# Nine zero products instead of 13 at TensorE's first place, and another order table, in a fused attention and max-of-three expert kernel

## The chip, the cores and the metric

The kernel runs on one core of a Trainium2 chip. The metric is the device time of one execution in microseconds; the time before is the median of three runs. One execution was also taken by the hardware profiler, and all rows below are of that one.

In the rows PE is TensorE (its products), PEld its weight loads, DVE is VectorE, ACT is ScalarE, POOL is GpSimd and SP is SyncE, which here only issues transfers. L719 is line 719 of the kernel.

## What is computed

Causal attention for 4 batches of 12 heads (448 tokens, 64 numbers a head), and then, for all 1792 tokens, the largest of three products with weight matrices, times an output matrix:

```python
scores = scale * np.matmul(q, k.transpose(0, 1, 3, 2))
scores = np.where(mask, -1000000000.0, scores)
scores = scores - np.max(scores, axis=-1, keepdims=True)
attn = np.exp(scores)
attn = attn / (np.sum(attn, axis=-1, keepdims=True) + 1e-09)
attn_out = np.matmul(attn, v)
...
x = attn_out.transpose(0, 2, 1, 3).reshape(B * S, H * D)
h = np.maximum(np.maximum(x @ w1, x @ w2), x @ w3)
return h @ w_out
```

## The kernel before

**Attention.** The 48 heads are taken as 24 pairs, six to a batch, and each pair's causal scores in two halves (7 blocks of 64 queries: three blocks in half a, four in half b). A half passes through these steps, each recorded once by a helper with its own line:

- L719, PE: scores into `S` (two buffers, `S0` for halves a and `S1` for halves b), 10 or 12 products in 32 bits, after a mask written as a small product.
- L743, DVE: the largest score of each row, one reduction a block into `acc`.
- L751 or L753: these, scaled, as the bias of the exponential, on ACT, DVE or POOL.
- L761, ACT: one exponential a block, from `S` into a staging tile (`region0`), with the row sums beside it.
- In the first six pairs (batch 0, "plain"): L774, PE transposes the result into `M` (three buffers), L541 on ACT moves it out of `M`; L901, PE spreads the inverse row sums into `M`; L847, PE multiplies with the values into `O`; L906 and L541 write `x`, the experts' input.
- In later pairs the exponentials are split in two 16-bit halves (L541 on ACT, L543 and L552 on DVE or POOL), transposed by a transfer (L829), and multiplied at L847.

**Weights.** Each of the 24 blocks of 128 rows is loaded (L935), brought into a 32-bit tile (L541 or L545), given its bound (L953, L950, L956, L960 on DVE) and split into two 16-bit halves (L541 or L545, and L561). L642 and L561 do the like for the values.

**Experts.** Batches 0 and 1 take L1041 (three products of 18 each for a column block, the largest of them kept at L1056) and L1472 (the output product). Batches 2 and 3 together take a scheme with seven products for eight (L1273, folds at L1286), whose sums and splits DVE prepares (L1126, L1131, L1317, L561, L543), and end with L1398, folds at L1414 and L1430, and stores.

**The order.** Each step is handed to a recorder (`add`) with the engines that may take it and a planned cost. `ORDER` lists the 1,973 steps by number in the order in which they are placed, and `ENGINE` names for each step the engine that takes it, two letters a step. The planner (`forward`) gives each a planned start by these two tables, and the steps are then issued in the order of planned starts, engine by engine. An engine runs its list strictly in that order, so the tables decide both who does a step and what stands ahead of it. The planner keeps PE's planned starts half a microsecond behind their inputs from planned time 90 on (`PAD`, `PAD_FROM`).

**The start.** Before the recorded steps, L1528 clears a tile `junk`, and L1532 multiplies it with itself into `S0`, 13 times, 384 columns each. Nothing reads the result. The first scores come next on PE; they need the first load of `qk` (L698, on SP's queue), the first thing that SP issues.

Of the kernel before, what the change touches and what calls it, by code (L numbers as in the profile page):

```python
# [34 lines left out]
ORDER = [15, 16, 17, 18, 19, 28, 29, 20, 977, 978, 50, 21, 30, 31, 32, 33, 0, 24, 22, 983, 23, 85, 2, 34, 979, 4, 6, 35, 51,  # L35
# [166 lines left out]
class Order:  # L202
# [89 lines left out]
    def forward(self, prio):  # L292
# [25 lines left out]
        while ready:  # L318
            cand = []
            for i in [ORDER[len(placed)]] if ORDER else ready:  # L320
                o = ops[i]
# [121 lines left out]
def attention_moe(ctx: ExitStack, tc: tile.TileContext, both_, v, w1, w2, w3, wo, out):  # L443
# [1087 lines left out]
    for _ in range(13):  # L1531
        PE.matmul(buf["S"][0][:, 0:384], junk[:, 0:P], junk, start=True, stop=True)  # L1532
# [86 lines left out]
```

## Time and profile before

| | |
|---|---|
| median of 3 runs | 436.81 us |
| the runs | 436.71, 436.81, 437.38 us |
| the profiled execution's own time | 436.95 us |
| its span, first to last instruction | 434.9 us |
| PE busy | 424.0 us, 97% |
| DVE busy | 400.0 us, 92% |
| ACT busy | 300.4 us, 69% |

The span lies 2.05 us below the time of the same execution; what lies around the span is not in the rows. Busy time counts an instruction from its recorded start to its recorded end, and where instructions overlap, once. The recorded ends of PE are modelled, and an instruction's recorded time on ACT or DVE is some tenth of a microsecond longer than the step from its start to the next one's, so steps from start to start are the price of one in a row.

### The profile page before, as it was taken

The page shows a single profiled execution, that of the slowest core. Times are in us where ns is not written, and L with a number is a line of the kernel's source. Part 1 is how long each engine was busy: PE and PEld are TensorE (multiplying, and loading weights), DVE is VectorE, ACT ScalarE, POOL GpSimd, SP SyncE. Part 2 cuts the span into 40 slices and gives each one's busy share as a digit, 9 for nine tenths or more (in the row PEclk, how much of TensorE's full clock was granted, in tenths as well). Part 3 has the DMA queues.
Part 4 walks back from the last instruction along what each step waited for, and adds up shares of the span by engine and source line. Part 5 has one row for each costly group of instructions (what it writes and reads, how often), then busy time and mean ns, then how long its engine had stood idle before and what let it go on. Part 6 is the DMA issues. An engine that isn't in the chain of part 4 may idle for free.

```text
span 434.9 us, 10858 instructions
## 1 busy us (share of the span) xinstructions
PE 424.0 (97%) x4286; PEld 245.4 (56%) x4286; DVE 400.0 (92%) x850; ACT 300.4 (69%) x738; POOL 119.9 (28%) x123
## 2 busy tenths in 40 slices
PE   7899899999999999999999999999999999999997
PEld 3677665656655555555555555555555555555554
DVE  4999999999999999986657889999999999999994
ACT  4999999799879899987679887964323422431530
POOL 2234443235451515232232332110130121131000
PEclk9999999999999999999999999999999999999999
DMA  8685589999999588476977567661000000000024
GB/s 314 209 310 176 207 238 245 221 232 211 253 246 247 181 222 161 93 161 110 200 162 173 138 142 121 98 133 51 2 0 21 2 1 23 0 2 0 2 98 155
DMA packets 87490, 60.46 MB, mean 139 GB/s; under 512 B 76304, under 2 KB 79504, under 8 KB 87440
## 3 DMA queue, kind: packets, MB, share of 16 engines
q1 hardware_dynamic: 83904, 48.14, 46.3%
q10 hardware_dynamic: 3536, 11.63, 8.0%
q8 instruction: 33, 0.54, 0.5%
q14 instruction: 17, 0.14, 0.1%
HBM read 35.39 MB, written 5.51 MB: 94 GB/s over the span
## 4 chain that ended last, share of the span: by engine, by line
PE 90%; ACT 8%; DVE 1%; issue 1%; POOL 0%; POOLq 0%; ACTq 0%
PE M L1041 29%; PE L L1273 14%; PE M L1472 10%; PE S L719 8%; PE O L847 7%; PE M L1273 7%; PE L L1398 5%; ACT region L761 4%; PE O L1273 4%; ACT region L541 2%; PE M L1398 2%; PE M L901 1%; PE O L1398 1%; ACT junk L642 1%; PE S L1532 1%; PE M L774 1%
## 5 line engine op out<-in xcount | busy, mean ns | idle before, releaser
L1041 PE MATMUL M<-x,w 128*128 128x448 f16 x648 | 127.1, 353 | 0.0
L1041 PEld LDWEIGHTS <-w 128*128 128x128 f16 x648 | 61.5, 98 | 56.8 <-issue 1.7
L761 ACT ACTIVATE region<-S,acc 128x128 f32<-128x128 f32 (+6 forms) x168 | 78.4, 480 | 10.2 <-DVE region L552 3.2
L743 DVE TENSOR_REDUCE acc<-S 128x1 f32<-128x320 f32 (+6 forms) x168 | 62.6, 414 | 10.6 <-PE S L719 9.3
L541 ACT ACTIVATE region<-region 128x896 f16<-128x896 f32 (+3 forms) x72 | 57.7, 809 | 20.9 <-DVE region L1206 7.9
L552 POOL TENSOR_TENSOR region<-region 128x896 f16<-128x896 f32 x22 | 41.6, 1890 | 53.2 <-DVE region L953 14.0
L1273 PEld LDWEIGHTS <-region 128*128 128x128 f16 x324 | 31.7, 98 | 29.6
L541 ACT ACTIVATE region<-region,cols 128x384 f16<-128x384 f32 (+1 forms) x38 | 22.5, 612 | 35.3 <-DVE region L1131 26.2
L1126 POOL TENSOR_TENSOR region<-w 128x384 f32<-128x384 f16 x21 | 19.0, 913 | 96.1 <-PE L L1273 24.9
L719 PE MATMUL S<-region 64*64 64x192 f32 (+6 forms) x672 | 43.8, 379 | 0.0
L1472 PE MATMUL M<-h,w 128*128 128x448 f16 x216 | 42.2, 353 | 0.0
L847 PE MATMUL O<-region,region 128*64 128x128 f16 (+3 forms) x1320 | 41.0, 219 | 0.0
L1273 PE MATMUL L<-region,region 128*128 128x448 f16 x189 | 37.7, 352 | 0.0
L1273 PEld LDWEIGHTS <-w 128*128 128x128 f16 x243 | 23.6, 98 | 21.9
L761 ACT ACTIVATION_READ_ACCUMULATOR region<-S,acc 128x1 f32 x168 | 35.6, 212 | 0.0
L1273 PE MATMUL M<-x,w 128*128 128x448 f16 x162 | 33.0, 353 | 0.0
L541 ACT ACTIVATE region<-region,acc 128x448 f32<-128x448 f32 (+6 forms) x59 | 28.4, 513 | 5.7 <-DVE acc L810 5.7
L1472 PEld LDWEIGHTS <-w 128*128 128x128 f16 x216 | 20.7, 98 | 19.5 <-issue 0.6
L719 PEld LDWEIGHTS S<-region 64*64 64x64 f32 x672 | 24.5, 134 | 10.7 <-issue 8.6
L847 PEld LDWEIGHTS <-region 128*64 128x64 f16 x1080 | 26.6, 111 | 5.5 <-issue 5.2
L956 DVE SCALAR_TENSOR_TENSOR region<-region 128x768 int32<-128x768 int32 x24 | 23.0, 961 | 0.0
L960 DVE SCALAR_TENSOR_TENSOR region<-region 128x768 int32<-128x768 int32 x24 | 22.7, 951 | 0.1
(174 smaller groups left out, 736.5 us busy)
## 6 DMA issues: line engine op xcount, KB each, us to landing
region<-in_moe_w_dram SPq DMA_DIRECT2D x12, 768.0 KB, 4.7
region<-in_qk_dram SPq DMA_DIRECT2D x19, 448.0 KB, 4.5
region<-in_moe_w_dram ACTq DMA_DIRECT2D x6, 768.0 KB, 4.7
region<-in_v_dram SPq DMA_DIRECT2D x10, 384.0 KB, 6.0
region<-in_moe_w_out_dram SPq DMA_DIRECT2D x4, 768.0 KB, 5.6
region<-in_qk_dram ACTq DMA_DIRECT2D x5, 448.0 KB, 3.5
out_dram<-osb SPq DMA_DIRECT2D x10, 224.0 KB, 2.4
region<-in_moe_w_out_dram ACTq DMA_DIRECT2D x2, 768.0 KB, 5.0
```

The lines of the kernel that those rows point to most:

```text
L541: ACT.activation(o, i, AF.Copy, scale=f)
L552: ENG[eng].tensor_tensor(out=o, in0=i, in1=hi, op=ALU.subtract)
L719: PE.matmul(ap(o, dims[0], dims[1:], D * (h ^ g), D), l, r, start=start, stop=True, skip_group_check=True)
L743: DVE.tensor_reduce(out=T(acc)[:, at : at + 1], in_=T(S)[:, c : c + w], op=ALU.max, axis=AX.X, negate=True)
L761: ACT.activation(T(y)[:, c : c + w], T(S)[:, c : c + w], AF.Exp, bias=T(acc)[:, 16 + at : 17 + at], scale=0.125, accum_out=T(acc)[:, 8 + a ...
L847: PE.matmul(o, vt(j, vl, (2 * p + h) * D), i, start=n < 2, stop=True, skip_group_check=True)
L956: DVE.scalar_tensor_tensor(out=xi(), in0=word(0), scalar=29, in1=xi(), op0=ALU.logical_shift_right, op1=ALU.bitwise_or)
L960: DVE.scalar_tensor_tensor(out=xi(), in0=word(1), scalar=SIGN, in1=xi(), op0=ALU.bitwise_and, op1=ALU.bitwise_or)
L1041: PE.matmul(T(M)[:, 0:S_LEN], w16[j][:, kk, wl, fs], xx[:, kk % 3, xl], start=(kk == 0 and wl + xl == 0), stop=(kk == 5 and wl == 1))
L1273: PE.matmul(T(M)[:, 0:S_LEN], stat(c, wl), mov(c, xl), start=first and n == 0, stop=n == 8, skip_group_check=True)
L1398: PE.matmul(T(M)[:, t[0] : t[1]], stat[0](c, wl), mov[0](c, xl)[:, t[0] : t[1]], start=first and c + wl + xl == 0, stop=c == 2 and wl == 1 ...
L1472: PE.matmul(T(M)[:, 0:S_LEN], w16[3][:, f, wl, es], T(("h", b, f))[:, hl], start=(f == 0 and hl + wl == 0), stop=(f == 5 and wl == 1))
```

## The change

The loop at L1532 runs nine times instead of 13, and the two tables have new values. The recorded steps, their planned costs and all other code are the same. (The middle of both tables is left out.)

```diff
-ORDER = [15, 16, 17, 18, 19, 28, 29, 20, 977, 978, 50, 21, 30, 31, 32, 33, 0, 24, 22, 983, 23, 85, 2, 34, 979, 4, 6, 35, 51,
...
+ORDER = [15, 16, 17, 18, 19, 977, 28, 20, 21, 50, 29, 24, 30, 978, 22, 23, 31, 32, 979, 26, 33, 980, 34, 35, 0, 36, 983, 51,
...
     ACT.activation(osc[:, 0:1], junk[:, 0:1], AF.Exp)
-    for _ in range(13):
+    for _ in range(9):
         PE.matmul(buf["S"][0][:, 0:384], junk[:, 0:P], junk, start=True, stop=True)
```

What the tables do to the engines' lists is shown at two places. The first is ACT's list around the exponentials of half a of the seventh pair (`acc0`, `S0`; the 43rd to 45th of 168), whose end frees `S0` for half a of the eighth pair. The row above them is the last exponential of the sixth pair. Before:

```order
L761 ACTIVATE region0_61,acc1_67<-S1_92,acc1_67 128x192
L541 ACTIVATE region4_65<-M1_89,bsc_101 128x448
L892 ACTIVATE acc1_67<-acc1_67,osc_100 128x8
L541 ACTIVATE region1_62<-region1_62 128x768
L761 ACTIVATE region0_61,acc0_66<-S0_91,acc0_66 128x448
L761 ACTIVATE region0_61,acc0_66<-S0_91,acc0_66 128x384
L761 ACTIVATE region0_61,acc0_66<-S0_91,acc0_66 128x64
```

Now:

```order
L761 ACTIVATE region0_61,acc1_67<-S1_92,acc1_67 128x192
L751 ACTIVATE acc0_66<-acc0_66,osc_100 128x3
L541 ACTIVATE region0_61<-M0_88 128x512
L892 ACTIVATE acc1_67<-acc1_67,osc_100 128x8
L761 ACTIVATE region0_61,acc0_66<-S0_91,acc0_66 128x448
L761 ACTIVATE region0_61,acc0_66<-S0_91,acc0_66 128x384
L761 ACTIVATE region0_61,acc0_66<-S0_91,acc0_66 128x64
```

The weight tile's step of 768 columns (`region1`) has moved behind these exponentials, and a bias of three columns, which DVE or POOL had before, stands ahead of them.

The second is PE's list where the first expert products (L1041) stand. The scores above them are those of half b of the seventh pair (`S_92`) before:

```order
L719 MATMUL S_92<-region_65 64x128 x2
L719 MATMUL S_92<-region_65 64x256 x2
L719 MATMUL S_92<-region_65 64x320 x2
L719 MATMUL S_92<-region_65 64x192 x2
L901 MATMUL M_90<-ident,acc_67 64x64 x14
L1041 LDWEIGHTS w_0_93
L1041 MATMUL M_89<-x_68,w_0_93 128x448
```

and those of half a of the eighth (`S_91`), one half further, now:

```order
L719 MATMUL S_91<-region_65 64x448 x2
L719 MATMUL S_91<-region_65 64x384 x2
L719 MATMUL S_91<-region_65 64x64 x2
L774 MATMUL M_89<-ident,region_61 128x128 x4
L1041 LDWEIGHTS w_1_94
L1041 MATMUL M_90<-x_68,w_1_94 128x448
```

The first expert products have moved behind one more half of scores and the last transposes of batch 0.

## Rows read from the trace of the kernel before

**Rows 1.** The page: busy time of each engine, with its share and its instructions.
```profile
PE 424.0 (97%) x4286; PEld 245.4 (56%) x4286; DVE 400.0 (92%) x850; ACT 300.4 (69%) x738; POOL 119.9 (28%) x123
```

**Rows 2.** Busy time by stretch; after the bounds their length, then each engine.
```profile
core 0: us, PE busy (x) PEld busy (x) DVE busy (x) ACT busy (x) POOL busy (x), PEclk, DMA share, GB/s
5.00:10.00 5.00, 3.15 (x50) 1.79 (x52) 3.37 (x10) 2.15 (x10) 1.21 (x2) 1.00 1.00 408
...
10.00:50.00 40.00, 35.32 (x584) 27.14 (x577) 39.16 (x92) 39.82 (x122) 15.66 (x22) 1.00 0.67 223
50.00:432.00 382.00, 381.74 (x3649) 214.68 (x3647) 356.26 (x738) 256.94 (x608) 101.85 (x92) 1.00 0.53 126
300.00:420.00 120.00, 120.00 (x636) 62.04 (x634) 119.02 (x218) 44.47 (x78) 20.36 (x22) 1.00 0.02 7
...
200.00:220.00 20.00, 20.00 (x264) 11.71 (x262) 12.36 (x34) 15.04 (x46) 3.71 (x6) 1.00 0.93 180
220.00:240.00 20.00, 20.00 (x248) 11.75 (x247) 13.15 (x29) 16.26 (x44) 6.58 (x6) 1.00 0.70 162
```

**Rows 3.** PE's waits over the span: for whom, us in total, times, longest.
```profile
PE M L774 <- ACT region L761: 2.4, 2, 1.7
PE M L774 <- ACT region L541: 1.2, 3, 0.8
```

**Rows 4.** The chain that ended last: start, length, what.
```profile
9.23 2.21 ACT region L761 x11
...
49.77 0.66 PE M L774 x4
...
54.26 1.24 PE M L1041 x6
```

**Rows 5.** Timeline of the first microseconds: start, length, what, idle before it.
```profile
0.79 0.40 SPq L698 DMA_DIRECT2D region<-in_qk_dram  x1
...
1.18 4.33 PE L1532 MATMUL S<-junk 128*128 128x384 f16 x13 [1.18 <-DVE junk L1528]
...
4.36 0.15 PEld L1532 LDWEIGHTS <-junk 128*128 128x128 f16 x1 [0.17 <-issue]
4.68 0.15 PEld L1532 LDWEIGHTS <-junk 128*128 128x128 f16 x1 [0.17 <-issue]
...
5.50 0.96 PE L719 MATMUL S<-region 64*64 64x448 f32 x12
...
6.56 2.41 DVE L743 TENSOR_REDUCE acc<-S 128x1 f32<-128x448 f32 x7 [4.67 <-PE S L719]
```

**Rows 6.** Transfers issued from 0.5 to 1.2 us: size, us to landing.
```profile
region<-in_qk_dram SPq DMA_DIRECT2D x1, 448.0 KB, 3.5
```

**Rows 7.** Timeline of ACT alone, 44 to 58 us.
```profile
44.19 1.01 ACT L541 ACTIVATE region<-region,bsc 128x768 f16<-128x768 f32 x1
45.02 0.71 ACT L761 ACTIVATE region<-S,acc 128x448 f32<-128x448 f32 x1
...
52.21 0.41 ACT L892 ACTIVATE acc<-acc,osc 128x8 f32<-128x8 f32 x1
52.40 1.04 ACT L541 ACTIVATE region<-region 128x768 f32<-128x768 f32 x1
53.25 0.71 ACT L761 ACTIVATE region<-S,acc 128x448 f32<-128x448 f32 x1
...
54.61 0.30 ACT L761 ACTIVATION_READ_ACCUMULATOR region<-S,acc 128x1 f32 x1
```

**Rows 8.** Timeline of PE alone, 49 to 58 us.
```profile
55.48 0.96 PE L719 MATMUL S<-region 64*64 64x448 f32 x12
56.43 1.18 PE L774 MATMUL M<-ident,region 128*128 128x128 f32 x8
```

**Rows 9.** DVE's instructions by line and form: busy, mean ns, idle before.
```profile
L561 DVE SCALAR_TENSOR_TENSOR w<-region,wf,w 128x768 f16<-128x768 f32 x22 | 22.0, 1006 | 0.0
...
L543 DVE TENSOR_SCALAR osb<-M,osc 128x448 f32<-128x448 f32 x3 | 2.0, 682 | 3.3 <-PE M L1472 3.3
```

More of the change, by code (lines that the diff above doesn't have):

```diff
@@ L33 @@
 V_FIRST = 14
-ORDER = [15, 16, 17, 18, 19, 28, 29, 20, 977, 978, 50, 21, 30, 31, 32, 33, 0, 24, 22, 983, 23, 85, 2, 34, 979, 4, 6, 35, 51,
[93 rows of a table removed]
+ORDER = [15, 16, 17, 18, 19, 977, 28, 20, 21, 50, 29, 24, 30, 978, 22, 23, 31, 32, 979, 26, 33, 980, 34, 35, 0, 36, 983, 51,
[93 rows of a table added]
     1972]
 ENGINE = (
-    "spacspdvspacpospacdvpedvdvdvdvsppedvdvdvacacacacpeacpeacpedvdvdvdvdvacacacacpeacpeacpeacdvpeacdvacposppedvdvdvac"
-    "acacacpeacpeacpedvdvdvdvpoacacacacpeacpeacpepodvpeacdvacposppedvdvdvpoacacacpeacpeacpedvdvdvdvdvacacacacpeacpeac"
-    "pepodvpeacdvacposppedvdvdvpoacacacpeacpeacpedvdvdvdvpoacacacacpeacpeacpeacdvpeacdvacposppedvdvdvpoacacacpeacpeac"
-    "pedvdvdvdvacacacacacpeacpeacpepodvpeacdvacposppedvdvdvpoacacacpeacpeacpedvdvdvdvdvacacacacpeacpeacpeacdvpeacdvac"
-    "pospacspacspacspacdvpedvdvdvdvacdvacdvacdvpoacdvsppedvdvdvdvacacacacposppedvdvdvdvacacacacacacposppepeacdvpeacdv"
-    "acposppedvdvdvacacacacacposppedvdvdvdvacacacacacacposppepepodvpeacdvacposppedvdvdvacacacacacposppedvdvdvdvacacac"
-    "acacacposppepeacdvpeacdvacposppedvdvdvacacacacacposppedvdvdvdvdvacacacacacposppepeacdvpeacdvacposppedvdvdvpoacac"
-    "acacposppedvdvdvdvacacacacacacposppepeacdvpeacdvacpoacpedvdvdvacacacacacposppedvdvdvdvacacacacacacposppepeacdvpe"
-    "acdvacpospacacacspacacacdvpedvdvdvdvacpoacdvacdvacdvacacspacspacspacdvpedvdvdvdvacpoacdvpodvpodvdvacpedvdvdvacac"
-    "acacacdvacacacacdvsppedvdvdvdvpoacacacacacdvacacacacacposppepeacdvsppedvdvdvacacacacacdvacacacacposppedvdvdvdvac"
-    "acacacacdvdvacacacacacposppepedvdvacpedvdvdvacacacacacdvacacacdvposppedvdvdvdvpoacacacacpodvacdvacdvacposppepeac"
-    "dvsppedvdvdvdvacacacpodvacdvacacposppedvdvdvdvdvacacacacacdvdvacdvdvdvdvsppepedvdvsppedvdvdvdvacacacpodvacacacac"
-    "dvsppedvdvdvdvacacacacacpodvacdvdvdvacposppepeacdvacpedvdvdvdvacacacpodvacdvdvdvdvsppedvdvdvdvacacacacacacdvacdv"
-    "acacacdvsppepeacdvsppedvdvdvpoacacacacdvacdvdvacdvsppedvdvdvdvpoacacacacacdvdvacacacdvposppepeacdvsppedvdvdvpoac"
-    "acacdvdvacacdvacdvsppedvdvdvdvacacacacacacdvacacacacacdvsppepeacdvacpedvdvdvacacacacacdvacacacacdvsppedvdvdvdvac"
-    "acacacacpodvdvacdvdvacposppepeacdvsppedvdvdvacacacacdvdvacacdvdvdvsppedvdvdvdvacacacacacpodvdvdvacdvdvposppepeac"
-    "dvsppedvdvdvdvacacacacdvacdvacdvdvsppedvdvdvdvpoacacacacdvdvacacacacacdvsppepeacdvsppedvdvdvdvacacacacdvacacacac"
-    "dvsppedvdvdvdvacacacacacdvdvdvacacacacdvsppepeacdvsppodvdvdvdvsppodvdvdvdvsppodvdvdvdvpedvdvdvdvdvpodvpodvpoposp"
-    "podvdvdvdvsppodvdvdvdvspacdvdvdvdvpedvdvdvdvdvacdvacdvpodvspacdvdvdvdvspacdvdvdvdvspacdvdvdvdvpedvdvdvdvdvacdvac"
-    "dvacdvacacdvdvdvdvspacdvdvdvdvacacdvdvdvdvpedvdvdvdvdvacdvacdvacdvacacdvdvdvdvacacdvdvdvdvspacdvdvdvdvpedvdvdvdv"
-    "dvacdvacdvacdvacacdvdvdvdvspacdvdvdvdvacacdvdvdvdvpedvdvdvdvdvacdvacdvacdvspacdvdvdvdvacacdvdvdvdvacacdvdvdvdvpe"
-    "dvdvdvdvacdvacdvacpospacdvdvdvdvspacdvdvdvdvspacdvdvdvdvpedvdvdvdvacdvdvdvdvdvdvacacacacacacpepepeacpepepedvpepe"
-    "pedvacpopepepeacpepepedvpepepedvacpopepepeacpepepedvpepepedvacpopepepeacpepepedvpepepedvacpopepepeacpepepedvpepe"
-    "pedvacpopepepeacpepepedvpepepedvacpodvpepepedvsppepepeacsppepepedvsppepepeacsppepepeacsppepepeacacpepepeacpepepe"
-    "dvpepepedvacdvpepepeacpepepedvpepepedvacdvpepepeacpepepedvpepepedvacpopepepeacpepepedvpepepedvacdvpepepeacpepepe"
-    "dvpepepedvacdvpepepeacpepepedvpepepedvacpodvpepepeacsppepepeacsppepepeacsppepepeacacpepepedvacpepepeacacdvdvpopo"
-    "dvpodvdvacdvacdvpodvacdvacdvdvdvpodvdvdvacdvacdvdvpoacdvacdvdvdvdvdvdvdvacdvacdvdvdvacdvacdvdvdvdvdvdvdvacdvacdv"
-    "dvdvacdvacdvdvdvdvdvdvdvacdvacdvdvdvacdvacdvdvdvdvdvdvdvacdvacdvpodvacdvacdvpodvdvpodvdvacdvacdvdvdvacdvacdvpopo"
-    "podvdvdvacdvacdvdvdvacdvacdvdvdvdvpodvdvacdvacdvdvdvacdvacdvpopodvdvdvdvacdvacdvpodvacdvacdvpodvpodvdvdvacdvacdv"
-    "podvacdvacdvpodvdvdvdvdvacdvacdvdvdvacdvdvdvpopopopodvdvacdvacdvdvdvacdvacdvdvpopodvdvdvacdvacdvdvdvacdvacdvpodv"
-    "podvdvdvacdvacdvdvdvacdvacdvpeacpedvpedvpedvpedvpepedvdvpeacpedvpedvpedvpedvpepedvdvdvdvdvpeacpedvpedvpedvpedvpe"
-    "pedvdvdvdvdvdvdvacdvacdvdvdvdvacdvacdvdvdvdvacdvpeacpedvpeacpedvpedvpepedvdvpeacpedvpedvpedvpedvpepedvdvdvdvdvpe"
-    "acpedvpedvpedvpedvpepedvdvdvdvdvacdvacdvacdvdvdvdvacdvacdvacdvdvdvdvpeacpedvpeacpedvpedvpepedvdvpeacpedvpedvpedv"
-    "pedvpepedvdvdvdvdvpeacpedvpedvpedvpedvpepedvdvdvdvdvacdvacdvacdvdvdvdvacdvacdvacdvdvacdvdvpepeacpepedvpepeacsppe"
-    "pedvpepedvacpepedvacpepedvacpepeacpepedvpepeacacpepedvpepedvacpepedvsppepedvsppepeacpepedvpepeacsppepedvpepedvsp"
-    "pepedvspdvpepedvsppepedvsp")
@@ new lines @@
+    "spacspdvspacpospacdvpedvdvdvdvsppedvdvdvacacacacpeacpeacpedvdvdvdvpoacacacacpeacpeacpedvdvpeacdvacposppedvdvdvac"
+    "acacacpeacpeacpedvdvdvdvpoacacacacpeacpeacpepodvpeacdvacposppedvdvdvpoacacacpeacpeacpedvdvdvdvpoacacacacpeacpeac"
+    "peacdvpeacdvacposppedvdvdvpoacacacpeacpeacpedvdvdvdvacacacacacpeacpeacpeacdvpeacdvacposppedvdvdvpoacacacpeacpeac"
+    "pedvdvdvdvdvacacacacpeacpeacpeacdvpeacdvacposppedvdvdvpoacacacpeacpeacpedvdvdvdvdvacacacacpeacpeacpeacdvpeacdvac"
+    "pospacspacspacspacdvpedvdvdvdvpodvacdvacdvpoacdvsppedvdvdvacacacacacposppedvdvdvdvpoacacacacacposppepeacdvpeacdv"
@@ new lines @@
+    "acposppedvdvdvacacacacacposppedvdvdvdvdvacacacacacposppepeacdvpeacdvacposppedvdvdvpoacacacacposppedvdvdvdvacacac"
+    "acacacposppepeacdvpeacdvacposppedvdvdvpoacacacacposppedvdvdvdvacacacacacacposppepeacdvpeacdvacpoacpedvdvdvacacac"
+    "acacposppedvdvdvdvacacacacacacposppepeacdvpeacdvacpoacpedvdvdvdvacacacacposppedvdvdvdvpoacacacacacposppepeacdvpe"
+    "acdvacdvspacacacspacspacdvpedvdvdvdvacpoacdvacdvacdvspacspacspacspacdvpedvdvdvdvacpopodvacdvacdvdvacpedvdvdvacac"
+    "acacacdvacdvacacposppedvdvdvdvacacacacacacdvacacacacacposppepedvdvsppedvdvdvdvacacacacdvacacacacposppedvdvdvdvac"
@@ new lines @@
+    "acacacacdvdvacdvdvacacposppepeacdvsppedvdvdvacacacacpodvdvdvacacdvsppedvdvdvdvacacacacacacdvdvacdvdvacdvsppepeac"
+    "dvsppedvdvdvpoacacacdvdvdvdvdvdvposppedvdvdvdvdvacacacacpodvacdvdvdvdvdvsppepedvdvsppedvdvdvacacacacacdvdvdvdvdv"
+    "dvsppedvdvdvdvacacacacacacdvdvdvacacacposppepedvdvsppedvdvdvacacacacpodvacdvacdvdvsppedvdvdvdvacacacacacdvdvdvac"
+    "acacacdvsppepedvdvsppedvdvdvdvacacacpodvacdvacdvdvsppedvdvdvdvacacacacacacdvacdvdvacacposppepeacdvsppedvdvdvdvac"
+    "acacacdvacdvacdvdvsppedvdvdvdvacacacacacacdvdvacacacacposppepedvdvsppedvdvdvdvacacacacdvacacacacdvsppedvdvdvdvac"
@@ new lines @@
+    "acacacacpodvacacacdvacposppepeacdvsppedvdvdvacacacacacdvdvacacacdvsppedvdvdvdvpoacacacacacdvacacacdvacdvsppepeac"
+    "dvsppedvdvdvdvacacacdvdvacacacacdvsppedvdvdvdvacacacacacpodvacacdvdvacdvsppepeacdvacpedvdvdvdvacacacdvdvdvacacac"
+    "dvsppedvdvdvdvacacacacacacdvacacacacacdvsppepeacdvsppodvdvdvdvsppodvdvdvdvsppodvdvdvdvpedvdvdvdvdvpodvpodvpoposp"
+    "podvdvdvdvsppodvdvdvdvspacdvdvdvdvpedvdvdvdvdvacdvacdvpodvspacdvdvdvdvspacdvdvdvdvspacdvdvdvdvpedvdvdvdvdvacdvac"
+    "dvacdvspacdvdvdvdvspacdvdvdvdvacacdvdvdvdvpedvdvdvdvdvacdvacdvacdvacacdvdvdvdvacacdvdvdvdvacacdvdvdvdvpedvdvdvdv"
@@ new lines @@
+    "dvacdvacdvacdvacacdvdvdvdvspacdvdvdvdvacacdvdvdvdvpedvdvdvdvdvacdvacdvacdvspacdvdvdvdvspacdvdvdvdvacacdvdvdvdvpe"
+    "dvdvdvdvacdvacdvacpospacdvdvdvdvspacdvdvdvdvspacdvdvdvdvpedvdvdvdvacpoacdvpodvdvacacacacacacpepepeacpepepedvpepe"
+    "pedvacpopepepeacpepepedvpepepedvacpopepepeacpepepedvpepepedvacdvpepepeacpepepedvpepepedvacpopepepeacpepepedvpepe"
+    "pedvacpopepepeacpepepedvpepepedvacpodvpepepedvsppepepeacsppepepedvsppepepedvsppepepeacsppepepedvacpepepeacpepepe"
+    "dvpepepedvacdvpepepeacpepepedvpepepedvacpopepepeacpepepedvpepepedvacdvpepepeacpepepedvpepepedvacpopepepeacpepepe"
@@ new lines @@
+    "dvpepepedvacpopepepeacpepepedvpepepedvacpodvpepepeacacpepepeacacpepepeacsppepepeacacpepepeacacpepepeacspdvdvpopo"
+    "dvdvdvdvdvdvacdvpodvdvdvdvdvdvpodvdvpodvacdvacdvdvdvacdvacdvdvdvdvdvdvdvacdvacdvdvdvacdvacdvdvdvpodvdvdvacdvacdv"
+    "dvdvacdvacdvdvdvdvdvdvdvacdvacdvdvdvacdvacdvdvdvdvpodvdvacdvacdvdvdvacdvacdvdvpodvpodvdvacdvacdvdvdvacdvacdvpodv"
+    "dvdvdvdvacdvacdvdvdvacdvacdvdvpopopodvdvacdvacdvdvdvacdvacdvpodvdvpodvdvacdvdvdvpodvacdvacdvdvpopopodvdvacdvacdv"
+    "podvacdvacdvpodvdvpodvdvacdvacdvpodvacdvacdvpodvdvpodvdvacdvacdvpodvacdvacdvpodvpopodvdvacdvacdvdvdvacdvacdvpodv"
@@ new lines @@
+    "dvdvdvdvacdvdvdvpodvacdvacdvpeacpedvpeacpedvpedvpepedvdvpeacpedvpedvpedvpedvpepedvdvdvdvdvpeacpedvpedvpedvpedvpe"
+    "pedvdvdvdvdvacdvacdvacdvdvdvdvdvdvacdvacdvdvacdvpeacpedvpeacpedvpedvpepedvdvpeacpedvpedvpedvpedvpepedvdvdvdvdvpe"
+    "acpedvpedvpedvpedvpepedvdvdvdvdvacdvacdvdvdvpodvdvacdvacdvacdvdvacdvpeacpedvpeacpedvpedvpepedvdvpeacpedvpedvpedv"
+    "pedvpepedvdvdvdvdvpeacpedvpedvpedvpedvpepedvdvdvdvdvacdvacdvdvdvdvdvdvacdvacdvdvdvdvacdvdvpepeacpepedvpepedvsppe"
+    "pedvpepedvsppepedvsppepedvsppepeacpepedvpepeacacpepedvpepedvacpepedvsppepedvacpepeacpepedvpepeacacpepedvpepedvsp"
@@ L168 @@
+    "pepedvspdvpepedvacpepedvac")
 PLAIN = 6
```

186 rows, old and new, of the table ORDER are left out of this document.

## The prediction

> **What bounds the kernel now.** I read the page first. PE is busy for 424.0 of 434.9 us [rows 1], so 10.9 us are the most that an order can give back if the work stays. Then I read the busy time by stretch, to find where those lie. From 50 to 432 PE is busy for 381.74 of 382 us; behind 432 there are 2.9 us, which hold the last evictions and stores; so before 50 some 7.7 us are idle [rows 2]. From 10 to 50 PE has 35.32 of 40, while ACT has 39.82 and DVE 39.16 [rows 2]: the first 50 us belong to ACT, with DVE close behind, and the rest to PE. The list of waits agrees: PE's longest are for ACT's exponentials (2.4 us) and for ACT's moves out of `M` (1.2 us) [rows 3]. The chain shows the change of hands. It runs through ACT's exponentials, takes the transposes at 49.77, which had waited for ACT, and stays on PE from there, with the first expert products (L1041) at 54.26 [rows 4].
>
> So the end is set by two things: how early PE has its queue filled for good (about 50 us now), and whether it has to wait again after that. What is gained ahead of that point comes off the end one for one. Nothing can be gained behind it except in the last 2.9 us, whose steps (two folds of half a tile, two stores) are of the same kind in the changed list.
>
> The sum is made against the profiled execution's own 436.95 us, which is 0.14 above the median of the runs.
>
> **The four products.** [...] Thirteen of them from 1.18 end at 5.34, and the first scores start at 5.50 [rows 5]. These took 0.96 us, as much as the same form at 55.48 [rows 8], so they already ran at the upper level; it rose somewhere between the last zero product's start and 5.50, and I take 5.4. What else the first scores need is the first `qk` load, issued at 0.79 [rows 5] and landed 3.5 us later [rows 6], at 4.29. So it was the zero products that held them. Nine end at 1.18 + 9 x 0.32 = 4.06; the load then comes last, and with the same 0.16 us of step the scores start at 4.45, 1.05 earlier.
>
> How much of that reaches DVE depends on the level. If it still rises at 5.4, the 0.95 us until then do half their worth (0.48), the other 0.48 follows, and the half ends at 5.88 where it ended at 6.46: 0.6 us gained. If it stays low, the half takes 1.92 and ends at 6.37, which gains 0.1. If the scores did not care for the level, all 1.05 come. I take 0.6 and keep 0.1 and 1.05. DVE's first maximum, which sat idle 4.67 us for these scores [rows 5], is next on the chain, then ACT's first exponentials, so this 0.6 shifts the stretch that ACT bounds as a whole, as long as the loads behind it (the weight tile, the values) are not what it then waits for.
>
> **The order at the front.** I counted both lists up to the 45th exponential, the last of the seventh pair's half a, since its end frees `S0`, for which PE's list now waits ahead of its first expert products. ACT has 94 instructions up to there in both lists. Two steps of 768 columns have left this stretch: one like that at 44.19 (0.83 to the next start) and that at 52.40 (0.85) [rows 7]. A small row-sum step (like that at 52.21, 0.19) [rows 7] and a bias, which I price the same, have come in. That is 1.68 - 0.38 = 1.3 us less ACT work ahead of this point. DVE, up to the maxima of the same half, has one split of a weight block less, 1.0 at most [rows 9], and otherwise the same within 0.1. With the start that is 1.9 us earlier by ACT and 1.6 by DVE.
>
> What PE makes of it: the 45th exponential ended at 54.9 [rows 7] and would end at 53.0. PE then has a half of scores (0.96) and four transposes, half of the 1.18 for eight [rows 8], and stands at 54.6 where it had done all attention work of that place. Before, it stood there at 57.61 [rows 8], but had done six expert products in 1.24 us [rows 4] as well: 56.4 without them. So 1.8 us by ACT, 1.5 by DVE. Moving the expert products back costs nothing by itself as long as PE waits there no longer than it did; their cover, to fill PE's waits for ACT, is what is given up, and the price if the exponentials come no earlier is just that 1.24 us.
>
> Behind this, the same instructions are left for PE, and it has no idle time to lose. I take 1.4 for the whole lead: nearer to DVE's figure than ACT's, because DVE is as full as ACT there and PE takes its list strictly in order, and a little off for a new short wait. The bounds are 0.1 (the level stays low and the order gives nothing) and 1.05 + 1.3 = 2.35.
>
> **The rest of the tables.** Thirteen more scalings (L543, 57 for 44) stand on DVE, and ACT has fourteen fewer (L541). At 0.68 each [rows 9] DVE gets at most 8.8 us more; some sums (L1126) have left it for POOL. By their place in the list eleven of the thirteen have come in between the 112th and the 126th of the 168 score maxima, and so around 200 us, where DVE is idle for 40 - 12.36 - 13.15 = 14.5 us [rows 2]. I cost them at nothing, under that cover. If the cover is gone, they cost up to 8.8, since from 300 to 420 DVE has only 1.0 us idle [rows 2] to catch up in.
>
> [...] With a rise at the old moment the start gives 0.6, with a later one 0.1 and the first rival below.
>
> **The rivals.**
>
> *The level rises later.* The first two halves of scores, 0.96 each, would take 3.84 from 4.45 and end at 8.3, not at 7.4: 0.9 late. PE's 3.15 busy us between 5 and 10 [rows 2] would need 6.3, so PE becomes the bound for as long as the level is low, and slips by up to 1.3. That eats the order's 1.3 and leaves 436.4 to 436.9. For it: the level was low until the thirteenth product at least. [...] Chance 0.15.
>
> *The lead is given back.* ACT and DVE are both nearly full in the front, and what was moved behind the 45th exponential has to be done soon after. If PE then waits for it once, as it now does at 49.77 (0.8 us, the longest of its waits for `M` [rows 3]), 0.8 of 1.4 is gone: 436.2. Against it stands that PE has expert products to fill in from there. Chance 0.22.
>
> *DVE becomes late: slower.* If the extra scalings meet a DVE that waits in the middle for PE's own scores, part of its 14.5 us cannot be used. If only half can (7.2), 8.8 - 7.2 = 1.6 us go into the stretch from 300, less the 0.6 of the start: PE then waits for folds, ends 1.0 us later than before, and the time is 437.8. It decides from the point where less than 8.2 of the 14.5 can be used. For it: DVE's share falls there just because it is fed by PE. Against it: the count of 8.8 is a bound from above, and the sums that left DVE for POOL are not in it. Chance 0.15.
>
> **How the numbers follow.** My forecast has a chance of 0.45: a lead of 1.0 to 2.0, time 436.95 - 1.4 - 0.14 = 435.4, its own range 434.8 to 435.9. A lead above 2.0 (up to 2.35, 434.4) has 0.03. What measurement of this kernel can tell from no change is about 0.2%, 0.87 us, so faster means below 435.9. Faster: 0.45 and 0.03, and a little of the given-back case, 0.50 in all. Same: the most of the given-back case and of the low level, 0.31. Slower: the DVE case and the low level where it lasts beyond 15 us, 0.19. The range runs from 434.2 to 437.6; it leaves out the better part of the DVE case (0.12) and about 0.05 below.
>
> **What would show it.** In the changed profile the first scores should start at 4.3 to 4.6 and end before 6.0 (right for the load and the level), or take nearly 1.9 us (the level rises later). The 45th exponential should end at 53.0 to 53.4, and PE's first expert product start near 54.6; PE should have less than 7 us idle before 50 to 55 and no wait above 0.3 behind it. DVE should be busier by several us around 200 to 240 and no later in its folds. I am wrong if PE's first scores start at 5.4 again, if the 45th exponential ends after 54, or if PE's list of waits has rows behind 60 us that add up to over 0.5.

## The result, and the profile after

The changed kernel takes 440.25 us (median of 14 runs, 436.89 to 442.81), the kernel before 437.05 beside it: ratio 1.0066, 95% interval 1.005 to 1.0082 (the two medians alone give 1.0073). It is slower by 0.66%; the forecast was 435.4, and 437.6 the upper end of its range. The profiled execution takes 439.56 with a span of 437.8 us; of before it was 436.95 and 434.9. Of all the runs below one, among the twelve of e4, took 492.19 us at a mean clock of 0.852; it is left out of e4's ratio and counted in its median.

First the page's busy row as in [rows 1], then the busy time by stretch as in [rows 2]: bounds and length, each engine, the granted clock, the DMA share and GB/s.

```profile
PE 424.1 (97%) x4282; PEld 245.7 (56%) x4282; DVE 405.9 (93%) x860; ACT 294.3 (67%) x727; POOL 124.1 (28%) x125
```

```profile
10.00:50.00 40.00, 35.17 (x604) 27.75 (x599) 39.46 (x94) 39.62 (x123) 16.68 (x22) 1.00 0.67 227
...
60.00:70.00 10.00, 9.66 (x84) 5.23 (x77) 9.82 (x23) 8.47 (x21) 2.89 (x2) 1.00 0.94 189
70.00:80.00 10.00, 7.77 (x60) 3.93 (x60) 7.85 (x18) 7.57 (x15) 4.28 (x3) 0.83 0.79 200
80.00:120.00 40.00, 40.00 (x593) 24.62 (x591) 37.69 (x80) 34.55 (x82) 14.72 (x11) 1.00 0.94 220
...
200.00:220.00 20.00, 20.00 (x249) 11.56 (x247) 17.50 (x55) 11.64 (x39) 3.72 (x3) 1.00 0.66 148
220.00:240.00 20.00, 20.00 (x264) 12.02 (x263) 16.90 (x39) 16.23 (x49) 6.57 (x6) 1.00 0.81 167
```

PE is full from 80 us on, as it was before. The loss lies between 69.6 and 77: PE is busy for 9.66 of the 10 us ahead of 70, and for 7.77 of the 10 behind it, at a mean clock of 0.83. PE's list of waits has a new second row against [rows 3] (the five waits of its first row all lie before 52 us):

```profile
PE S L719 <- ACT region L761: 3.1, 5, 0.9
PE M L580 <- ACT hacc L541: 2.6, 1, 2.6
PE M L774 <- ACT region L761: 1.6, 1, 1.6
...
PE M L774 <- ACT region L541: 0.9, 2, 0.6
```

PE's timeline there (start, length, what, idle time before and what ended it), and then the busy time of the stretch behind the wait:

```profile
69.20 0.46 PE L901 MATMUL M<-ident,acc 128*64 128x64 f32 x10
72.23 0.33 PE L580 MATMUL M<-ident,wmx 128*128 128x128 bf16 x3 [2.57 <-ACT hacc L541]
...
73.52 1.71 PE L719 MATMUL S<-region 64*64 64x128 f32 x16
```

```profile
73.58:77.00 3.42, 3.42 (x25) 1.58 (x23) 3.42 (x12) 2.61 (x6) 3.27 (x3) 0.50 0.46 102
```

PE waits 2.57 us for a bank of `M` that the activation into `hacc` frees; and 1.35 us after it goes on, at 73.58, the granted clock falls to 0.50, the lower of the two levels in this trace's clock records (1.00 and 0.50), for 3.42 us. At half the speed this costs half of them, 1.71, by estimate (the 16 score products at 73.52 took 1.71 us; in e1 below they take 0.95). Together that is 4.28 us; the two versions below that have neither, e1 and e2, are 4.1 and 4.2 us faster than the changed kernel. What was late shows in ACT's own timeline:

```profile
67.02 0.65 ACT L541 ACTIVATE hacc<-M,wr 128x448 f32<-128x448 f32 x1
68.40 0.92 ACT L541 ACTIVATE region<-region 128x768 f32<-128x768 f32 x1 [0.72 <-DMA region<-in_moe_w_dram]
68.46 2.98 ACTq L623 DMA_DIRECT2D region<-in_v_dram  x1
71.54 0.63 ACT L541 ACTIVATE hacc<-M,wr 128x448 f32<-128x448 f32 x1 [2.22 <-issue]
```

ACT's sequencer issues a load of values (L623, from `values()`) on its own queue, and this issue alone takes 2.98 us. In the kernel before the same issue stands at 68.65 and takes 0.34:

```profile
68.59 0.93 ACT L541 ACTIVATE region<-region 128x768 f32<-128x768 f32 x1
68.65 0.34 ACTq L623 DMA_DIRECT2D region<-in_v_dram  x1
...
69.91 0.65 ACT L541 ACTIVATE hacc<-M,wr 128x448 f32<-128x448 f32 x1
```

What the load has to wait for in the changed kernel, the split on DVE that frees its buffer, had ended at 67.73, 0.73 us before the row of this issue starts (68.46). So something other than data held it. SP issued a load meanwhile at the usual price:

```profile
69.14 0.33 SPq L935 DMA_DIRECT2D region<-in_moe_w_dram  x1
```

### The profile page after: what moved, and what is told of

It is laid out like the page before. It is cut to its first block, busy times and chain, and to the rows that moved or that the text cites. A ratio compares the mean times of both kernels' runs of the same rounds, so it can differ in the third digit from the quotient of the medians.

```text
span 437.8 us, 10849 instructions
## 1 busy us (share of the span) xinstructions
PE 424.1 (97%) x4282; PEld 245.7 (56%) x4282; DVE 405.9 (93%) x860; ACT 294.3 (67%) x727; POOL 124.1 (28%) x125
## 4 chain that ended last, share of the span: by engine, by line
PE 84%; ACT 10%; DVE 3%; issue 2%; POOL 1%; ACTq 0%; POOLq 0%
PE M L1041 26%; PE L L1273 14%; PE M L1472 9%; PE S L719 7%; PE M L1273 7%; PE O L847 6%; PE L L1398 5%; ACT region L761 4%; PE O L1273 4%; ACT region L541 3%; PE M L1398 2%; PE M L901 1%; ACT junk L642 1%; DVE acc L743 1%; PE O L1398 1%
## 5 line engine op out<-in xcount | busy, mean ns | idle before, releaser
L1041 PE MATMUL M<-x,w 128*128 128x448 f16 x648 | 127.8, 354 | 0.0
L1041 PEld LDWEIGHTS <-w 128*128 128x128 f16 x648 | 61.8, 98 | 58.0 <-issue 3.3
L743 DVE TENSOR_REDUCE acc<-S 128x1 f32<-128x384 f32 (+6 forms) x168 | 63.5, 415 | 8.4 <-PE S L719 8.2
L552 POOL TENSOR_TENSOR region<-region 128x896 f16<-128x896 f32 x21 | 39.5, 1889 | 50.7 <-DVE region L953 13.5
L1126 POOL TENSOR_TENSOR region<-w 128x384 f32<-128x384 f16 x25 | 23.1, 928 | 100.4 <-DVE region L561 35.8
L541 ACT ACTIVATE region<-region,cols 128x384 f16<-128x384 f32 (+1 forms) x35 | 20.9, 616 | 36.7 <-DVE region L1131 18.6
L719 PE MATMUL S<-region 64*64 64x192 f32 (+6 forms) x672 | 45.1, 387 | 0.0
L761 ACT ACTIVATION_READ_ACCUMULATOR region<-S,acc 128x1 f32 x168 | 36.7, 219 | 0.0
L719 PEld LDWEIGHTS S<-region 64*64 64x64 f32 x672 | 25.1, 136 | 11.3 <-issue 9.2
L541 ACT ACTIVATE region<-region,acc 128x64 f32<-128x64 f32 (+6 forms) x52 | 23.4, 489 | 4.2 <-DVE acc L810 4.0
```

Of the source, the lines that this page charges most:

```text
L541: ACT.activation(o, i, AF.Copy, scale=f)
L552: ENG[eng].tensor_tensor(out=o, in0=i, in1=hi, op=ALU.subtract)
L719: PE.matmul(ap(o, dims[0], dims[1:], D * (h ^ g), D), l, r, start=start, stop=True, skip_group_check=True)
L743: DVE.tensor_reduce(out=T(acc)[:, at : at + 1], in_=T(S)[:, c : c + w], op=ALU.max, axis=AX.X, negate=True)
L761: ACT.activation(T(y)[:, c : c + w], T(S)[:, c : c + w], AF.Exp, bias=T(acc)[:, 16 + at : 17 + at], scale=0.125, accum_out=T(acc)[:, 8 + a ...
L1041: PE.matmul(T(M)[:, 0:S_LEN], w16[j][:, kk, wl, fs], xx[:, kk % 3, xl], start=(kk == 0 and wl + xl == 0), stop=(kk == 5 and wl == 1))
```

## The experiments

Theory A was that this issue itself, on this queue, is slow (it is the first of ACT's queue here, and comes right behind a transpose). The rival, theory B, is that ACT had run out of instructions. It came from the DMA records of the trace, which call two queues "instruction" and show 33 transfers of 16 KB on the one and 18 of 8 KB on the other within the span of after; that these bring the engines' own programs is read from the name. On one of them a transfer (8 KB) starts at 69.56 and ends at 69.98, just where the packets of the transpose end (69.8), and ACT's sequencer goes on at 71.48.

**e1: that load on SP's queue.** One entry of the table of engines:

```diff
+ENGINE = ENGINE[: 2 * 454] + "sp" + ENGINE[2 * 454 + 2 :]
```

> The changed kernel with one transfer moved: the load of v that ACT's queue issues at 68.46 us, and that holds ACT for 2.98 us, goes to SP's queue, behind the transposes there. Theory A (the issue of this transfer, from ACT's queue, is what holds ACT): ACT goes on at 69.3, the 2.57 us wait of TensorE at 69.65 us and the half clock from 73.58 to 77.00 are gone together, and the time is 440.25 - 2.57 - 1.6 = about 436.1, 0.998 of the kernel before. Theory B (ACT has run out of instructions: the instruction queue's transfer starts only at 69.56, when the packets of the transposes end, and ACT goes on at 71.48): ACT stands until about 71.4 all the same, now in front of an ACTIVATE, TensorE's wait stays near 2.5 us, and the time stays near 440.2, 1.0066 of the kernel before.

Measured: 436.11 us, 0.9973 of before (0.9961 to 0.9986). The row of 2.98 is gone, `hacc` starts at 69.74, PE waits 0.2, and the score products behind it run at the upper level (0.95 us for the 16 that had taken 1.71):

```profile
70.41 0.33 PE L580 MATMUL M<-ident,wmx 128*128 128x128 bf16 x3 [0.20 <-ACT hacc L541]
...
71.71 0.95 PE L719 MATMUL S<-region 64*64 64x128 f32 x16
```

As theory A had it. ACT's instruction transfer started even later here (71.59), and ACT did not stand still, which speaks against B:

```profile
69.74 0.62 ACT L541 ACTIVATE hacc<-M,wr 128x448 f32<-128x448 f32 x1
70.26 0.94 ACT L541 ACTIVATE region<-region 128x896 f16<-128x896 f32 x1
71.10 0.41 ACT L761 ACTIVATE region<-S,acc 128x192 f32<-128x192 f32 x1
```

**e2: sixteen idle activations at the start.** The order of everything else stays.

```diff
-    ACT.activation(osc[:, 0:1], junk[:, 0:1], AF.Exp)
+    for _ in range(17):
+        ACT.activation(osc[:, 0:1], junk[:, 0:1], AF.Exp)
```

> The changed kernel with 16 more activations of one column at the very start, where ACT waits from 2.3 to 7.1 us anyway (they need about 3 us there). They leave the order of all else as it is, and put every later instruction of ACT 16 places further on in its program. Theory A (the issue itself): ACT's transfer at 68.46 takes 2.98 us as before, and the time stays near 440.2 (1.0066 of the kernel before). Theory B (instructions arrive late): ACT asks for its next block of instructions 16 instructions earlier, near 62 us, ahead of the loads and transposes, the transfer takes 0.34 us, and the time falls to about 436.1 (0.998). A third case, B for TensorE too (its own instruction transfer starts at 69.56 as well and ends 70.8): ACT is not held, but TensorE's wait at 69.65 us stays near 2.5 us, then without ACT as its releaser, and the time stays near 440.2.

Measured: 436.02 us, 0.9976 (0.9964 to 0.9988). The same issue, still the first on ACT's queue, behind the same transpose, takes 0.38:

```profile
68.49 0.92 ACT L541 ACTIVATE region<-region 128x768 f32<-128x768 f32 x1 [0.75 <-DMA region<-in_moe_w_dram]
68.55 0.38 ACTq L623 DMA_DIRECT2D region<-in_v_dram  x1
69.31 0.61 ACT L541 ACTIVATE hacc<-M,wr 128x448 f32<-128x448 f32 x1
```

Theory A falls. On that instruction queue a transfer now starts at 55.84, and none between 60 and 75: since only ACT's program has grown, the one at 69.56 was ACT's. (On the other instruction queue, with transfers of 16 KB, which I take for PE's, one starts at 69.52 here too, and holds nobody.) But e1 had spoken against B. What fits both is theory C: **an issue on ACT's own queue is held as long as ACT's own instruction transfer is outstanding**; other work of ACT is not. When ACT asks for a transfer stands in no record, so "outstanding" is inferred from when the transfer lands.

**e3 and e4: the two parts of the change alone.** e3 has the tables of after with 13 zero products (its edit is shown), e4 the tables of before with nine.

```diff
-    for _ in range(9):
+    for _ in range(13):
```

> The changed kernel with 13 products of zeros again, so the tables alone. By the forecast the four products are worth 0.6 us at the start: 440.25 + 0.6 = 440.9 if the wait at 69.65 stays what it was (both theories A and B, if 0.6 us of lag at the start moves the transfers and the instructions together). If it comes out near 437, the wait hangs on a coincidence of a fraction of a us and not on the order of the tables.

> The kernel before with nine products of zeros, so the start alone. By the forecast 437.05 - 0.6 = 436.4 (0.9985 of the kernel before); the rival there was 436.9 (a later rise of the clock at the start). If it comes out above 437.5, an earlier start by itself brings a collision like that at 69.65 us.

Measured: e3 442.29 us, 1.0114 (1.0094 to 1.0135); e4 436.45, 0.9984 (0.9973 to 0.9995). The start is worth 0.55 to 0.7 us, as forecast. The loss is in the tables, and it is no coincidence of a fraction of a us: e3 even lies above the 440.9 expected, and with the start 1.3 us later the issue is held for 4.25 us (70.44 to 74.69), and the instruction transfer comes at 73.04, again where the packets of the transpose end (73.1).

**e5: four idle activations.** As e2, with `range(5)`.

> The changed kernel with only 4 more activations at the start (the run with 16 had ACT's instruction transfer at 55.84 instead of 69.56, and no wait). Theory B (ACT stands because it has run out of instructions, behind the 201st row of ACT): the place where it runs out moves 4 rows forward, to the exponentials and the hacc activation at 66.6 to 67.0, ahead of the load of v; the load's own row is 0.34 to 0.39. Theory C (ACT does not run out; an issue on ACT's own queue is held as long as an instruction transfer of ACT's is outstanding): the rows up to the load run as before and the load's row at about 68.5 is again near 3 us if the instruction transfer is again late. In both the time is then about 440; if 4 rows are enough to bring the instruction transfer ahead of the transposes (they start moving data at 65.2), row and wait are gone and the time is near 436.1.

Measured: 439.85 us, 1.0068 (1.005 to 1.0086).

```profile
66.91 0.65 ACT L541 ACTIVATE hacc<-M,wr 128x448 f32<-128x448 f32 x1
67.42 0.92 ACT L541 ACTIVATE region<-region 128x768 f32<-128x768 f32 x1
67.61 4.00 ACTq L623 DMA_DIRECT2D region<-in_v_dram  x1
71.72 0.63 ACT L541 ACTIVATE hacc<-M,wr 128x448 f32<-128x448 f32 x1 [3.38 <-issue]
```

The place where ACT stands did not move by four rows; it is the issue again, and it ends as before 1.35 us behind the instruction transfer (69.95 to 70.26). Theory B, which had a fixed place in ACT's list, falls; C fits.

**e6: the load one step later,** behind the `hacc` that PE waits for.

```diff
-1000, 272, 454, 1225, 291,
+1000, 272, 1225, 454, 291,
```

> The changed kernel with the load of v one step later in the order table, still on ACT's queue: behind the hacc activation that TensorE waits for, no longer ahead of it. Theory C: ACT reaches the load at about 69.4 instead of 68.5 and is held until the instruction transfer has landed (about 71.5, a row of about 2 us), but hacc is then done, so TensorE's wait of 2.57 us and the half clock go, and what is late is the next of ACT's work, 1 to 2 us of it, with at most some tenths at TensorE: 436.1 to 437.0. Theory B: ACT runs out of instructions behind its 201st row whatever that row is, here behind or at the hacc activation, and TensorE's wait stays near 2.5 us: about 440.

Measured: 440.48 us (437.19 to 441.46), 1.006 (1.0037 to 1.0082). The rows came as C had it, the time did not:

```profile
69.40 2.32 ACTq L623 DMA_DIRECT2D region<-in_v_dram  x1
69.49 0.61 ACT L541 ACTIVATE hacc<-M,wr 128x448 f32<-128x448 f32 x1
71.82 0.95 ACT L541 ACTIVATE region<-region 128x896 f16<-128x896 f32 x1 [1.73 <-issue]
```

```profile
73.22 0.25 PE L719 MATMUL S<-mr,ident 64*64 64x128 bf16 x4 [1.74 <-ACT region L761]
```

The issue is held for 2.32 us until 71.72, `hacc` is out in time, and the wait of L580 for it, which B expected with its 440, is gone. But an exponential now stands behind the held issue, and PE waits 1.74 us for the scores' bank, until 73.22. "At most some tenths" was wrong: at this place, too, something that PE needs soon stands behind the issue. The profiled execution (438.63) is at clock 1.00; in the eight runs above 439.9 the mean clock is 0.991 to 0.999, so the lower level may add to it there, which no profile here shows.

**e7 and e10: the tables alone without the held issue,** with 13 products and either the activations of e2 or the entry of e1.

> Tables alone without the wait: the changed kernel with 13 products of zeros and 16 more activations at the start. With nine products and the same activations it took 436.0; the start alone was worth 0.55 (436.45 against 437.0). If the parts add up: 436.6, 0.999 of the kernel before, so that the tables bring 0.4 and not the 0.8 of the forecast. If it comes out at 437.0 or above, the tables bring nothing even without the wait.

> Tables alone without the wait, in another way than by the activations: 13 products of zeros, and the load of v on SP's queue. The activations gave 437.25 (0.9997). If the tables are worth nothing: 437.0, within 0.1 per cent of the kernel before. If they are worth the 0.4 that the runs with nine products seemed to leave for them: 436.6, 0.999. Theory C again: no issue of ACT stands while its instruction transfer is outstanding, so there is no wait over 1 us behind 60 us.

Measured: e7 437.25 us, 0.9997 (0.9985 to 1.0009); e10 436.77, 0.9986 (0.9972 to 1.0). The tables bring between 0.1 and 0.6 us (437 x 0.0003 and x 0.0014); both intervals reach 1, so that the tables alone gain anything is not shown.

**e8: the reverse, in the kernel before:** its weight load at 61.50 moved from ACT's queue to SP's.

```diff
+ENGINE = ENGINE[: 2 * 1067] + "sp" + ENGINE[2 * 1067 + 2 :]
```

> The reverse: the kernel before (13 products, its own tables) with one transfer moved, the weight load that ACT's queue issues at 61.50 us, to SP's queue. ACT's instruction transfer, which started at 66.83 there while the transposes (66.2 to 70.4) were moving, then stands two rows further back in ACT's program, about 1 us later. Theories B and C, if it then falls behind the transposes' packets: it starts near 70.4, ACT's load of v at 68.65 (first transfer of ACT's queue now) becomes a row of about 3 us, TensorE waits 1 to 2.5 us and the time is 438.5 to 441. If it still gets in among the transposes: 437.0, no change, and a first transfer on ACT's queue is shown to cost nothing either.

Measured: 436.88 us, 1.0001 (0.9986 to 1.0016). The instruction transfer got in among the packets of the transpose (66.57, in 65.8 to 69.4), and the load, now the first on ACT's queue, took 0.40. That the first issue is slow is ruled out a second time; the wait itself was not brought about in the kernel before.

**e9: two transfers of SP's queue exchanged,** the weight load ahead of that of q and k. The kernel before has them in this order too, but with the weight load on ACT's queue.

```diff
-        last = None
+        last, z = None, [k for k, p in enumerate(self.placed) if p[2] in (350, 1067)]; self.placed.insert(z[1], self.placed.pop(z[0]))
```

> The changed kernel with two transfers of SP's queue in the other order, as the kernel before has them: the weight load (issued at 61.50) ahead of the load of q and k (60.71), both ahead of the second transpose; ACT's program is untouched. Theory C says only that an issue of ACT waits for ACT's instruction transfer; what makes that transfer late is open, and this run asks it. Theory D (it is late because the weight load's packets, 63.2 to 68.0, are still moving when it is asked for at about 66 and the transposes follow at once): the weight load's packets end near 65.7 as in the kernel before, the instruction transfer starts before 67.5 as there (66.83), the row of the load of v is 0.34 to 0.4 and the time is 436.1, 0.998. Theory E (any transfer asked for while a transpose is moving waits for its end, and the kernel before merely asked in time): the instruction transfer still starts near 69.6, the row is near 3 us and the time 440.

Measured: 440.42 us, 1.0058 (1.0039 to 1.0077). The weight's packets end at 66.3, and the instruction transfer still starts only at 70.90, with the end of the transpose's packets (70.9). Theory D falls. E has the time and the transfer of ACT right, but not as a rule for any transfer: in the same trace one of 16 KB on the other instruction queue starts at 68.53, in the middle of the transpose's packets (66.8 to 70.9).

All rows of the load side by side, in us, with the instruction transfer of ACT from the DMA records:

| execution | packets of the transpose | instruction transfer | the issue's row | its end behind the transfer's |
|---|---|---|---|---|
| after | 65.2 to 69.8 | 69.56 to 69.98 | 68.46 to 71.44 | 1.46 |
| e3 | 67.3 to 73.1 | 73.04 to 73.35 | 70.44 to 74.69 | 1.34 |
| e5 | 65.1 to 70.0 | 69.95 to 70.26 | 67.61 to 71.61 | 1.35 |
| e6 | 65.8 to 70.1 | 69.83 to 70.25 | 69.40 to 71.72 | 1.47 |
| e9 | 66.8 to 70.9 | 70.90 to 71.21 | 68.44 to 72.52 | 1.31 |
| before | 66.2 to 70.4 | 66.83 to 67.20 | 68.65 to 68.99 | not held |
| e8 | 65.8 to 69.4 | 66.57 to 66.88 | 68.33 to 68.72 | not held |
| e2 | 65.2 to 69.9 | 55.84 to 56.40 | 68.55 to 68.93 | not held |

Five held issues of different lengths end at one distance, 1.31 to 1.47 us, behind the end of the instruction transfer; three that come 1.4 us or more behind it take 0.34 to 0.40. e4 (transfer 65.67 to 65.98, row at 68.23 of 0.34) and e7 (57.49 to 58.06, row at 69.15 of 0.39) are not held either. Of all the loads and stores that ACT issues in the twelve profiles only these five take over 0.6 us. They also end 1.58 to 1.64 us behind the last packet of the transpose; but in before, e2, e4, e7 and e8 the issue went through in the middle of such packets, so the transpose alone does not hold it. What makes the transfer late stays open: in before and e8 it got in near the start of the same transpose, in the five held cases and e1 it came at its end, and in e10 it started at 69.24, 1.5 us ahead of the end.

## Why the prediction was wrong, step by step

**What bounds the kernel** was right: PE is full from 80 us to the end in both, and what the front gains comes off the end, as e4 and the pair e1 and e2 show.

**The four products** were right: scores at 4.25 (forecast 4.45), their half done before 6.0, worth 0.55 to 0.7 for the 0.6 of the sum (e4). The 0.32 us a product of the sum is the step of the weight loads in [rows 5], and after has it again (3.08 to 3.40). That the scores do half their worth ahead of 5.4 was my estimate, which no run shows by itself: the first scores took 0.96 in [rows 5], 1.48 in after and 1.77 in e4, and the 16 score products above 1.71 at a clock of 0.50 for 0.95 in e1. The clock records of the trace begin with 1.00, at 5.32 in the profile of after and at 5.38 in before; taking this for the rise, the first rival did not come there. In e4's profile they begin only at 6.93, and DVE's first maximum still started 0.42 us earlier than in [rows 5] (6.14 for 6.56), where the sum had 0.1 for a late rise. That fewer zero products make the rise later does not show: with nine this moment lies between 3.89 (e9) and 7.06 (e6), with 13 between 4.25 (e10) and 7.13 (e3).

**The order at the front** was right in its rows and too big in its sum. The 45th exponential ended at 53.20 (forecast 53.0). The scores that wait for it start at 53.51, 2.0 us earlier than in [rows 8], and the first expert products at 55.22 (forecast 54.6):

```profile
53.51 0.96 PE L719 MATMUL S<-region 64*64 64x448 f32 x12
54.72 0.66 PE L774 MATMUL M<-ident,region 128*128 128x128 f32 x4 [0.26 <-ACT region L541]
55.22 1.11 PE L1041 MATMUL M<-x,w 128*128 128x448 f16 x5
```

At this place the kernel before stood as follows:

```profile
54.19 1.31 PE L1041 MATMUL M<-x,w 128*128 128x448 f16 x6
55.43 0.25 PE L719 MATMUL S<-mr,ident 64*64 64x64 bf16 x4
...
57.44 2.43 PE L1041 MATMUL M<-x,w 128*128 128x448 f16 x12
```

Up to 57.44 there and up to 55.22 here PE has done the same products, but for the six expert products at 54.19 (1.24 us to the next start) and the four zero products. Its lead is therefore 57.44 - 1.24 - 55.22 = 0.98 us, where the sum had 1.8 by ACT and 1.5 by DVE and took 1.4. The transposes end at 55.38, 0.8 later than the sum's 54.6: the exponential ended 0.2 later, 0.3 passed from its end to the scores, which the sum put at nothing, and the transposes met a new wait of 0.26 for ACT.

PE's idle time from 10 to 50 did not shrink: 40 - 35.17 = 4.83 us for the 4.68 of [rows 2]. Its waits changed place. Those of the transposes (L774) fell from 3.6 us [rows 3] to 2.5, but those of the scores (L719) rose to 3.1 us in five waits, where the kernel before has

```profile
PE S L719 <- ACT region L761: 0.4, 2, 0.2
```

Without the held issue the tables bring 0.1 to 0.6 where the sum had 0.8, and the whole change 0.9 (by the medians) to 1.2 (by the ratio of e1) for 1.4. The 436.1 and 436.0 of e1 and e2 lie just outside the forecast's own range of 434.8 to 435.9.

**The step that failed** is "Behind this, the same instructions are left for PE, and it has no idle time to lose", with "a little off for a new short wait" behind it. The rival "the lead is given back" priced such a wait by the longest of its kind in [rows 3], 0.8 us. The wait that came is 2.57, and behind it the clock was at 0.50 for 3.42 us: 4.28 us by the estimate above, more than the whole lead. It comes from a part of the tables that the sum never walked through: the transfers that ACT issues, and what stands behind them in ACT's list. The same load stood in ACT's list of the kernel before, three rows ahead of an activation into `hacc` that frees a bank of `M`. That its row could grow from 0.34 to 3 us no row of before showed; that PE's bank hung on an engine that also issues transfers could be read there. The prediction's own sign for this, rows of PE's waits behind 60 us that add up to over 0.5, was the one that came.

**The rest of the tables** was right: DVE is busy 17.50 and 16.90 of 20 us around 200 to 240 (12.36 and 13.15 in [rows 2]), and PE does not wait for it. The kernel did become slower, but not by the mechanism of that rival.

## What to carry to other kernels

The load that ACT issues here stood in ACT's own list, and while the issue took 2.98 us the activation behind it waited with it, 2.22 us: when an order is changed, walk the issues of each engine too, and see which bank or buffer the next steps behind each of them free. The issue that stalled although its data were ready (67.73 for 68.46) ended in all five held cases 1.31 to 1.47 us behind a transfer that the kernel's own text does not have; look for the instruction queue in the DMA records of the stretch, and try the transfer on an engine that computes nothing (e1: 436.11 us, 0.9973), or a few idle instructions at the start (e2: 436.02 us, 0.9976). These two versions beat both kernels here.

## What the runs showed of the hardware

- The DMA records call two queues "instruction", with transfers of 8 KB on the one that I take for ACT's (its transfer moved from 69.56 in after to 55.84 in e2, with sixteen more activations) and of 16 KB on the one that I take for PE's. ACT's started at 69.56 in after, 2.7 us later than in before, with the end of a transpose's packets, and an issue on ACT's queue took 2.98 us (2.3 to 4.3 in after, e3, e5, e6 and e9), while SP issued a load at 69.14 in 0.33. In before, e2, e4, e7 and e8 the transfer had ended 1.4 us or more ahead of the issue, which took 0.34 to 0.40.
- The granted clock fell to 0.50 for 3.4 us in the profiles of after, e3 and e5, behind idle times of PE of 2.57, 3.9 and 3.3 us; in e9 it stayed up behind one of 3.0, in e6 behind one of 1.74. Idle length alone does not decide it. Of the 14 runs of after, 13 show a mean clock of 0.992 to 0.996 and 439.2 to 442.8 us; the one with 1.000 took 436.89. The kernel before is not free of it: in 3 of its 75 runs beside e1 to e10 the mean clock is 0.996, at 438.4 to 438.8 us.
- With the same nine products at the start, the clock records begin with 1.00 at 5.32 in after and at 6.93 in e4, and the same first scores took 1.48 and 1.77 us: a few tenths of a us at the start that neither the tables nor the number of zero products is seen to decide.
